# One kernel, all its steps in another order

## The chip, the cores and the metric

The kernel runs on one core of a Trainium2 chip. The metric is the time of one execution in microseconds (us), as the device measures it. Of several executions the median counts.

## What is computed

Three parts follow each other on 8192 tokens of 192 numbers: a local attention over 7 neighbouring tokens, a gated feed-forward layer of width 1536, and a feed-forward layer of width 2048 with a rational activation. Everything is float32 at the outside; the weights arrive as 8-byte numbers.

```python
w = exp(weight_gen - max(weight_gen));  w = w / (sum(w) + 1e-09)      # 8 heads, 7 taps
x1 = sum over k of w[..., k] * x shifted by k                         # 2 x 4096 tokens, 192 wide
x2 = (sigmoid(x1 @ w_gate) * (x1 @ w_val)) @ w_out                    # width 1536
h  = x2 @ w_in                                                        # width 2048
g  = (a0 + a1 h + a2 h^2 + a3 h^3) / (1 + |b0 h| + |b1| h^2 + 1e-06)
out = g @ w_out2
```

## The kernel before

**Tiling.** The tokens are cut into 17 blocks: 15 of 512 tokens and two of 256. A block goes through attention, the first layer (12 units of 128 columns), and the second layer (16 units; the two short blocks take the units in pairs, 6 and 8 of them). Matmuls in the projections run on numbers that are split into a high and a low part, five matmuls for each product of 512 columns.

**Steps and letters.** Each piece of work is a step with a short name. A step does its work on one engine and hands the next step to a waiting list. The lists are first in, first out, so the name says which kind of work comes next, and the list says on which data.

- Weights come in 25 pieces. K loads one with DMAs on SyncE's (SP's) queue; Ka (ScalarE, L183) and Kd (VectorE, L187 to L193) turn the 8-byte words into float32; Kh (ScalarE, L367) and Kl (VectorE, L373) split them; Kc copies the part of the last 64 rows into the tile WT with four DMAs on SP's queue (L217). A projection needs the Kc of its piece.
- X loads a block's inputs on SP's queue; Na, Nb, Nc make the attention weights (Nb is the exponential on ScalarE). Seven steps B (VectorE, L283) make the products of a block, and six steps J or j sum them: **J** lets a transfer add one into the other (a DMA on GpSimd's queue, L430), **j** does it with a VectorE addition (L428). Z (ScalarE) and T1 (TensorE transposes, L459) follow the last of them, then C1 (ScalarE) and L1 (VectorE, L316).
- g and v are the two projections of the first layer into the PSUM banks pg and pv, which exist once each. S (sigmoid, ScalarE) frees pg, M (VectorE, L502) frees pv. G (ScalarE) is the high part of their product; the low part is **L** (a VectorE subtraction, L518) or **l** (ScalarE writes the negative, L515, and a GpSimd DMA adds, L516). O is the projection back. E, E1, E2, C2, L2 turn its sum into the second layer's input; in 14 blocks E2 is again a DMA that adds (L573).
- H is a unit's projection in the second layer (two PSUM banks h). A (three ScalarE instructions), V (L609), W (L614) on VectorE free the bank. **Q** adds two tiles with a GpSimd DMA (L625), **q** with VectorE (L623). R, U (ScalarE), T, Y, D (VectorE, L618), P (TensorE, L673) and F (ScalarE and the output DMA) end the block.

```python
def do_J_j(b, last, x1, to, t, eng):
    ...
    if eng is nc.gpsimd:
        nc.vector.tensor_add(out, out, in_)
    else:
        nc.gpsimd.dma_start(out=out, in_=in_, accum_op=ALU.add)
...
def do_L_l(b, c, g1, gh, eng):
    gl = tl(gp, "gl", [P, T], F32R)
    if eng is nc.gpsimd:
        nc.scalar.activation(gl, g1, AF.Identity, scale=-1.0)
        eng.dma_start(out=gl.bitcast(F32), in_=g1, accum_op=ALU.add)
    else:
        eng.tensor_sub(gl, g1, gh.bitcast(F32))
```

**What sets the order.** One string, ORDER, lists the names of all 3947 steps, and the program issues them in that order. Every engine and every queue works through its own instructions strictly in the order in which they were issued, and waits at one whose data or buffer is not there, whatever stands behind it. The string sets nothing else: buffers rotate as steps ask for them (four r tiles, five v tiles, four q tiles for weights and for the second layer alike).

Of the kernel before, what the change touches and what calls it, by code (L numbers as in the profile page):

```python
# [17 lines left out]
P = 128  # L18
D = 192
# [6 lines left out]
T = P * JB  # L26
# [19 lines left out]
S M K l v E j B g J O E1 M G E2 l G v B S M g C2 l O Kl v Ka S Kd g M Kh v S Kc B Kd K O L2 K g Kd K M Kl G H O G K Ka
L X S v J A g J O G L Z V Ka Ka W l S T1 M C1 G v Ka Kd O L1 Kd M K H H A G g l V v O S Kl Kc A g W H M S B G L g Kd V
v A W V S Q O R L O H U B W Kc B A g M V Q Kd R v H O S M G A Y v W g L G Ka Q U M L T V O S v M H E g W A E1 J v J D
S M Y H V A g Q v G V S W O T B l P E2 R W M H P J G U g L H B A V O A R W v J D Y V P C2 O W S H G l H Kd T M g A G S
P V U W Q g L2 D A H v S G R V L O W O A Na M B Q T V L P H v U Y D J W Y A V P g R S P G M H O A U g v G W S H Nb B L  # L50
P T V W J g D S M A v Nc V H M Z Q L A V W g S Q R v O G P W Y U T1 M X l v T M P C1 L1 O G H l R A D H A P T g V W B
B q S H G V v W A O J V W O Y R M D g G Q H S P v U L B M A g S H A V L v W g Y V T W M G O O D U S P P L R T G J E H
Q L E1 G L Y E2 g R v M H O v S g O A A V W U V S q B M P W D g T G U Y Y C2 J H P S O F A V v L2 H B W A D P P V H Q
G M R g W v L T H B O A G M A P V W R U J D U H S Q V W P L P H T j g l A B A S V W G V v R M Q X Y W P H O H U v D A
g O P R S Y Y T j P G V M L v W g A H M l V W v S G T D U A O Z M V g W v P T1 O G S L T C1 L1 P Q H l H Na R M Y g v
D P G A V U W S A B H O g Q O G D P V M A S G Q W T L B H B P g v V R l U A W V W R J M Y D l H S A V W O v M H Y T g
P G S H A O V A B g S v L W P Q g D U R G M V P W J E E1 Q L F H R v O M H S v T Y A V g W O D U H G S A j B M P U P
E2 L Y B G v Nb O O T L Q A V W P M G V R J P B g C2 L D H A O V G W v S Y W O l H T g P A Q M S H v U g D A S P V W T
V H g W L2 M J H J Y R A U V D v M P G A Q W Nc v S P G H O A T Q Z L M P V V W g v W S T1 P R Y C1 G M D L O L1 O H U
L g G v A X Q B V H L W P B R S Y H g A V M O O U v G A T L V W O H Y S g M R v W S E G g P S U B T D M E1 g L A H q v  # L60
P V G j J A W L O H T D S R E2 B P g Q U O Y G A R V M S v T G W P M L D H V W G L U Y v M O A g P Y H G S L J A v B g
Q M V V F S W W C2 v R O L2 J H A D H B U V P W P A H A M Y Q l V P g W V O P R T S W U H v D B A T J V Y G q G H A W
g M J X P O S T L D P H g V R Z A G W v H Q S M L V O W g U A L V v H P M S D T P R P W G O v U A V Q W T1 Y D G R O
C1 l U L1 T P H A g P B Q V W L B M H H T O S A V g W Y D G O v P B M L A H S R v U A Q O Y M g R S V v G W H J E D Y
P A M l g U V P P W G T S H B V g W E1 Y T Q E2 v Na G l H A V S M g L W R U J O P D G H A D A O V O C2 V W F v W H q
P S g A Y L2 H Q P S M J R V v T W P D A H L O V M U G A L W V v W R M H B Y g T P B J Nb v P S H A g V G D S j M P U
g G W A O v H Q T L S V W A R G B H M v O X Nc L P V U O g P M Q W L H A J G Y R L D v P V S W G A O M T V Q g W v Z
T1 G S Y O D C1 L1 P L l g H B U S M H g A S v A G V T Q g M W Y S R v B H V O D J L R A M P V W g U U W P O T H Y G O
S B A L H D g E G V W Q Y A Q E1 v S P V R H W U g M T P D v M A H R U A J O V L G P W G P Y T V H F O q A W L B P T R
V H v E2 L S A P U D O W M g B H V Y S v A P M g S G V v W H M L g Q J C2 A W v V M G S O g L2 G P H L Q W J v R B Y H  # L70
T O D M S A A G L V V P W O Q B g O P U W T J H D Y v H X R U P Y M A J S v V W A P T H V G D G g Z M Q L W A P V S L
W R v L T1 M Na C1 L1 R B O G P H D U B U Nb A O T O g L T V B J S P Y H v W A G g S Q V O H g Y A M W L S P R V H D v
A O g W D B M Q U E V H R W T v G Y A V J U W P M H Q S P D A H E1 L v g M Y V S v A G R Q V J W L T M B g S G O U P O
v G P Nc W L H A Y g V S L E2 H O A M F g V W G v T L D J M C2 P P S B g H R P D G O W U A V Q H B W T L2 v P L R S G
g A V S U H W g M Y Q A V H O v A R Y W U J P H V W D P T M O v G Q L j A H V G X R U M S D L v Y P A M W P Z g H O L
V v O W A V G W T1 C1 L P S G L1 T Q R P M H O Y g v A G V B H B U J W O Q T H D S M g A V P S g A L L q W v T M S O D
R G P R H O B A g V Y J U P v W P G D P V E W H M L E1 Y l v O G T H S P l A B g V D A M Q W v G S g F V O L H U P W Y
S R g T A H M U V S W v Q D O H g A j B M G v V B W A E2 R C2 S V M Y P J W T H P H B L L2 D O A V W G v L U Q X R g P
O Y G T S A M V H O W v P U A G g L S M H q V G A P j W Q J V g D R W H A Y S v H M V T P A v L P W g H O M Z Na U D V
W Q A O G V P W T S R v T1 L C1 R Y O L M L1 G D P O B H U g H S L G A Y O A B g V W v V H S Q g W P J A M U P T D G H  # L80
V L T R v P W Q A U V R P L H O S Y A M E v W g S D P H Y g V T W M G H P U A V T S W Y Q l A F B v E1 G R H Q U L g M
V W O v O D G E2 M A S V H W v A G O L D g B M L J q S P V Y v B W g T M j O C2 R P U H T O R S A H A B g D J v V V W
G L W G S P U P M L2 H A g J Q Y H A G S R V Q W Y V W v D P H l P B A M O H g j v A R V W T P P M L Q U H S V D v G W
A M T O U Z O g X v S Nb P V Y L W Y G M T1 P D C1 L1 G L O R Nc H g A S Q L V G H T A v U M O L g v S W H O D B T A O
E P M V R Q g W Y V P B v D E1 S J G H g U W A B H A S V R G M V B J W P E2 v P M T J Q L U g S v W H Y L G O C2 B P D
g G H P A M j v V L W L2 S A Y g M H F V T S W Q R D O A V P W v M U T H R A P B V Q W O U H g H G A v L S P L Y O G T
l g A S V Y P W j V g Q R D W U H O P A M G B l V T W H R v U j A D M H P O V S Y v W g H M O P G G D Z v A A V Y V W
W Q P H L R T S O M g A U S v V Q W T1 C1 L O P G M L1 D L H R g H G Y A v S T M V Q U P W O G D L G R P L g H v T A P
O V X W O S A U B E B M Y V L g W S H A V v T g H G Q E1 A S P P W M Q D v V R W B g Y J U H H A J L V Y S A E2 P P G
B O M v W g F V W M H S T v H D O A V M C2 W L L2 G g P S A q J L B D v R P H U G V O M W q G B A g H R U V O P W P A  # L90
T J Y R V H D S G L J v Q P W O H l Y U g T A M Na S v V W G g l A Y V P W S H H R D O T g A L U M Q V R S B v A G P M
J D v W P M V H g A W O Z T O V v W Y G S U T1 P P Nb L C1 Q L1 H M L H R G A g Q l v S O Nc V X W T M G D A O g S v Y
H V G D g O L S W M U B B A V O l E v G g S H M q P v g R J T Y D M R P P U W S G B E1 v H A A V M W Y L V B P W g T O
O S G Q v H M H E2 l U g L G R v A P Y V A W T V O H S P G W D U A M g C2 T V J D W Q F L2 J O H A Y S v R V P L H P W
H A Q U R P B A V W M G g U v H O L V O P D Q S T G B A L W g Y P J M l T S V H W R v A G D V B J P H W U g Q Y A V P
S M H P W A v D H O V A W X J M Q g Y v V W Z T D T1 L O S P M G R B P G P C1 L1 U R H H g T Y U D A O S G L v V W Q M
H A A V g W V v H S P R L B T U L O M W q Y R g B T J O H v Y G A O S L P P V E W A G H E1 D A V M J W g O l q v U S M
# [668 lines left out]
```

## Time and profile before

| what | value |
|---|---|
| median of 3 runs | 1396.8 us (1396.23 to 1398.79) |
| profiled execution, its own time | 1397.84 us |
| its span, first to last instruction | 1396.0 us |
| granted clock of TensorE, mean | 0.989 of full speed |
| instructions | 18221 |

Times below are in us from the span's start. TensorE is PE, its weight load PEld, VectorE DVE, ScalarE ACT, GpSimd POOL. The profile gives for each engine when it worked, how long it idled before an instruction, and what ended the idle time. A matmul of 512 columns overlaps the one before it, so a busy PE is an upper bound of the work it does.

### The profile page before, as it was taken

The numbers are of one execution on the slowest core, as the hardware profiler recorded it, in microseconds if no ns is written. First come the engines' busy times: TensorE is split into PE (matmuls) and PEld (weight loads), VectorE is DVE, ScalarE is ACT, GpSimd is POOL, SyncE is SP. The second block draws the span as 40 slices with busy tenths as digits, with TensorE's granted clock in tenths as the row PEclk, the third lists the DMA queues.
The fourth block names the chain that finished last, engine by engine and source line by source line (L and its number), as shares of the span: only waits on it lengthen the run. The fifth ranks groups of instructions, "written<-read, shape, count | busy, mean of one in ns | idle before, by whom it ended". The sixth has DMA issues, their size and how long they took to land.

```text
span 1396.0 us, 18221 instructions
## 1 busy us (share of the span) xinstructions
PE 1330.1 (95%) x6602; PEld 1150.1 (82%) x6602; DVE 1241.8 (89%) x1654; ACT 1203.7 (86%) x1820; POOL 233.8 (17%) x274
## 2 busy tenths in 40 slices
PE   1788999999999999999999999999999999999987
PEld 0566888888888888878888888888888888899986
DVE  6876998998999898989989999998988999899987
ACT  4665899889889988988989998999898999999985
POOL 1222211112111111111101011110112101211110
PEclk9999999999999999999999999999999999999999
DMA  9998565446535354554626255542555725454452
GB/s 222 236 227 196 100 132 101 84 99 129 111 68 133 72 113 93 106 114 76 142 43 138 48 113 109 94 111 54 101 104 96 146 52 108 83 108 84 95 108 59
DMA packets 59746, 153.82 MB, mean 110 GB/s; under 512 B 7436, under 2 KB 17162, under 8 KB 59656
## 3 DMA queue, kind: packets, MB, share of 16 engines
q0 software_dynamic: 38304, 108.54, 42.7%
q1 hardware_dynamic: 21064, 44.11, 10.4%
q8 instruction: 52, 0.85, 0.3%
q14 instruction: 38, 0.31, 0.1%
q10 hardware_dynamic: 288, 0.00, 0.0%
HBM read 31.51 MB, written 6.29 MB: 27 GB/s over the span
## 4 chain that ended last, share of the span: by engine, by line
PE 49%; DVE 5%; ACT 5%; issue 3%; DMA 2%; POOL 0%; POOLq 0%; ACTq 0%; DVEq 0%
PE acc L673 13%; PE h L295 3%; PE h L296 2%; PE h L297 2%; PE h L298 2%; PE h L299 2%; PE pv L295 2%; PE pg L296 2%; PE pg L295 2%; PE pg L297 2%; PE pg L298 2%; PE pg L299 2%; PE pv L296 2%; PE pv L297 2%; PE acc L533 2%
## 5 line engine op out<-in xcount | busy, mean ns | idle before, releaser
L673 PE MATMUL acc<-wo,v 128*128 128x192 f32 x2048 | 369.8, 327 | 4.1 <-DVE v L618 3.2
L673 PEld LDWEIGHTS acc<-wo,v 128*128 128x128 f32 x2048 | 343.6, 190 | 19.8 <-DVE v L618 4.5
L609 DVE TENSOR_TENSOR v<-v,h 128x512 f32<-128x512 f32 x256 | 174.9, 684 | 82.3 <-ACT r L602 80.8
L600 ACT ACTIVATE v<-h,co 128x512 f32<-128x512 f32 x256 | 176.5, 690 | 44.8 <-PE h L299 40.4
L625 POOL DMA_DIRECT2D q<-r x113 | 104.0, 921 | 604.2 <-ACT r L602 527.1
L614 DVE SCALAR_TENSOR_TENSOR v<-v,co,h 128x512 f32<-128x512 f32 x256 | 189.9, 744 | 3.8
L618 DVE SCALAR_TENSOR_TENSOR v<-v,co,r 128x1024 f32<-128x1024 f32 x128 | 163.3, 1278 | 1.1 <-ACT r L635 1.1
L602 ACT ACTIVATE r<-h 128x512 f32<-128x512 f32 x256 | 155.8, 609 | 2.7 <-DVE q L618 2.4
L601 ACT ACTIVATE q<-h 128x512 f32<-128x512 f32 x256 | 153.4, 599 | 4.7 <-DVE v L618 4.7
L630 ACT ACTIVATE r<-q,co 128x1024 f32<-128x1024 f32 x128 | 147.9, 1156 | 11.1 <-DMA q<-r 8.3
L618 DVE SCALAR_TENSOR_TENSOR v<-q,v 128x1024 f32<-128x1024 f32 x128 | 155.8, 1219 | 0.4
L618 DVE SCALAR_TENSOR_TENSOR q<-q,r 128x1024 f32<-128x1024 f32 x128 | 155.9, 1218 | 0.1
L502 DVE TENSOR_TENSOR sg<-sg,pv 128x512 f32<-128x512 f32 x192 | 130.8, 681 | 26.8 <-PE pv L299 16.4
L490 ACT ACTIVATE sg<-pg 128x512 f32<-128x512 f32 x192 | 116.3, 606 | 38.6 <-PE pg L299 22.1
L635 ACT ACTIVATE r<-r 128x1024 f32<-128x1024 f32 x128 | 136.4, 1068 | 0.9
L508 ACT CAST gh<-sg 128x512 fp32r<-128x512 f32 x192 | 119.4, 626 | 11.1 <-DVE sg L502 9.9
L430 POOL DMA_DIRECT2D x<-pr x78 | 79.2, 1016 | 264.7 <-DVE pr L283 110.3
L295 PE MATMUL h<-X2h,W0h 128*128 128x512 f32 (+1 forms) x272 | 117.0, 430 | 5.7 <-DVE v L614 2.8
L296 PE MATMUL h<-X2l,W0h 128*128 128x512 f32 (+1 forms) x272 | 103.5, 380 | 0.0
L297 PE MATMUL h<-X2h,W0l 128*128 128x512 f32 (+1 forms) x272 | 103.3, 380 | 0.0
L298 PE MATMUL h<-X2h,WT 128*128 128x512 f32 (+1 forms) x272 | 103.2, 379 | 0.0
L299 PE MATMUL h<-X2l,WT 128*128 128x512 f32 (+1 forms) x272 | 102.9, 378 | 0.0
(138 smaller groups left out, 2859.1 us busy)
## 6 DMA issues: line engine op xcount, KB each, us to landing
q<-r POOLq DMA_DIRECT2D x113, 512.0 KB, 4.6
x<-pr POOLq DMA_DIRECT2D x70, 384.0 KB, 5.6
gl<-sg POOLq DMA_DIRECT2D x57, 256.0 KB, 3.8
x<-in_x_dram SPq DMA_DIRECT2D x13, 960.0 KB, 5.5
out_dram<-pr SPq DMA_DIRECT2D x15, 384.0 KB, 3.1
v<-in_moe_w_out_dram SPq DMA_DIRECT2D x14, 384.0 KB, 4.8
r<-r SPq DMA_DIRECT2D x28, 128.0 KB, 2.4
r<-r POOLq DMA_DIRECT2D x14, 256.0 KB, 5.0
```

What stands on the lines that cost most here:

```text
L295: mm(d, W0h[:, w], h[:, 0, :], start=True, stop=False)
L296: mm(d, W0h[:, w], lo[:, 0, :], start=False, stop=False)
L297: mm(d, W0l[:, w], h[:, 0, :], start=False, stop=False)
L298: mm(d, WT[:, w], h[:, 1, :], start=False, stop=False)
L299: mm(d, WT[:, w], lo[:, 1, :], start=False, stop=True)
L600: nc.scalar.activation(v[:, e, :], ph, AF.Identity, scale=reg["a3"], bias=a2)
L601: nc.scalar.activation(q[:, e, :], ph, AF.Square, scale=reg["b1r"])
L602: nc.scalar.activation(a[:, e, :], ph, AF.Abs, scale=reg["b0"])
L609: nc.vector.tensor_mul(v, v, ph)
L614: nc.vector.scalar_tensor_tensor(out=v, in0=v, scalar=a1, in1=ph, op0=ALU.add, op1=ALU.mult)
L618: nc.vector.scalar_tensor_tensor(out=out, in0=in0, scalar=scalar, in1=in1, op0=op0, op1=op1, reverse0=neg)
L673: mm(acc[:, s // 2, (s % 2) * D:(s % 2 + 1) * D], g[:, (e * jb + s) * P:(e * jb + s + 1) * P], wo2[:, c, :], start=(c == 0 and s % 2 == 0) ...
```

## The change

The string ORDER is replaced by another order of the same steps. No function, tile or number elsewhere is touched. The counts of six names change, in pairs: of the block sums 7 go from J to j (82 and 20 before, 75 and 27 now); one low part goes from L to l (135 and 57 before, 134 and 58 now); one sum goes from Q to q (113 and 15 before, 112 and 16 now).

```diff
--- before.py
+++ after.py
@@ -38,75 +38,75 @@
 NB = len(BLOCKS)
 FOLD_PE = (0, NB - 2, NB - 1)
 ORDER = """
-Na Nb Nc K K Na root B B Ka B Ka J K B B B B J j J Kd Kh K J Ka K Kd Kl Ka K Kd Nb Kc Kd Kh Kh j Nc Z Ka X T1 C1 Kh Kd
...
+Na K K Nb Nc root Na B Ka B B B B B Ka K Kd Ka K B K Ka J j K j Kh Kd Kh J Kd Kl Kd Kh Kc Nb Nc Kh J j Kl X Z K T1 Kl
...
 """
```

The order of the instructions that the new string gives shows at three places what moved.

GpSimd's queue at the start of the program, before: four DMAs sum the first block's products (X2l, X2h and pr hold products, x1 the sum), and the low parts gl and the second block's sums follow.

```order
L430 DMA x1_0_138<-X2l_0_140 128x768
L430 DMA X2h_0_145<-X2l_1_156 128x768
L430 DMA X2h_1_158<-pr_1_162 128x768
L430 DMA x1_0_138<-X2h_0_145 128x768
L167 MEMSET x_0_231 128x384
L516 DMA gl_0_341<-sg_0_285 128x512
L430 DMA x1_0_297<-pr_1_318 128x768
L516 DMA gl_1_356<-sg_1_338 128x512
```

The same place now:

```order
L430 DMA x1_0_138<-X2l_0_143 128x768
L430 DMA X2h_1_149<-pr_1_176 128x768
L430 DMA x1_0_138<-X2h_0_145 128x768
L167 MEMSET x_0_231 128x384
L430 DMA x1_0_277<-pr_1_285 128x768
L430 DMA x1_0_277<-pr_0_321 128x768
L516 DMA gl_2_437<-sg_2_395 128x512
```

The sum of products 2 and 3 has left the queue (VectorE does it now), and the first two low parts have left it too.

SP's queue at the pieces of the first layer's last projections, before (v and q tiles are loads of weights, WT the copies of a Kc; WT from r_3_367, r_1_426 and r_3_529 serve units 6 and 7, 8 and 9, 10 and 11):

```order
L225 DMA v_2_429<-in_moe_w_out_dram 128x2x384
L217 DMA WT_81<-r_3_367 64x256 x4
L203 DMA v_3_505<-in_moe2_w_in_dram 128x512
L204 DMA q_3_506<-in_moe2_w_in_dram 64x512
...
L203 DMA v_4_556<-in_moe2_w_in_dram 128x512
L204 DMA q_0_557<-in_moe2_w_in_dram 64x512
...
L217 DMA WT_81<-r_1_426 64x256 x4
L217 DMA WT_81<-r_3_529 64x256 x4
```

The same pieces now (r_3_356, r_1_440 and r_3_514):

```order
L217 DMA WT_81<-r_3_356 64x256 x4
L225 DMA v_2_561<-in_moe_w_out_dram 128x2x384
L217 DMA WT_81<-r_1_440 64x256 x4
L203 DMA v_3_636<-in_moe2_w_in_dram 128x512
L204 DMA q_3_637<-in_moe2_w_in_dram 64x512
...
L217 DMA WT_81<-r_3_514 64x256 x4
L165 DMA x_0_711<-in_x_dram 128x1920
```

The copies for units 8 and 9 stood behind eight loads of the second layer's weights (two pieces of four DMAs) and stand ahead of them now; those for units 10 and 11 stand behind four of them.

VectorE where the second block's attention weights are normalized, before:

```order
L502 TENSOR_TENSOR sg_1_638<-sg_1_638,pv_0_669 128x512
L272 TENSOR_REDUCE red_1_239<-wn_1_238 128x64
L273 TENSOR_SCALAR red_1_239<-red_1_239 128x64
L274 RECIPROCAL red_1_239<-red_1_239 128x64
L275 TENSOR_TENSOR wn_1_238<-wn_1_238,red_1_239 128x448
L502 TENSOR_TENSOR sg_2_706<-sg_2_706,pv_0_710 128x512
```

The same place now:

```order
L502 TENSOR_TENSOR sg_0_608<-sg_0_608,pv_0_610 128x512
L272 TENSOR_REDUCE red_1_239<-wn_1_238 128x64
L273 TENSOR_SCALAR red_1_239<-red_1_239 128x64
L274 RECIPROCAL red_1_239<-red_1_239 128x64
L275 TENSOR_TENSOR wn_1_238<-wn_1_238,red_1_239 128x448
L428 TENSOR_TENSOR x1_0_277<-x1_0_277,pr_0_604 128x768
L502 TENSOR_TENSOR sg_1_632<-sg_1_632,pv_0_662 128x512
```

The second block's last sum is a VectorE addition now, and it stands in front of the step M (L502) that frees the bank pv. It adds to x1, into which a DMA of GpSimd's queue adds just before.

## Rows read from the trace of the kernel before

**Rows 1.** The page, part 1: busy time of each engine, its share, instructions.

```profile
PE 1330.1 (95%) x6602; PEld 1150.1 (82%) x6602; DVE 1241.8 (89%) x1654; ACT 1203.7 (86%) x1820; POOL 233.8 (17%) x274
```

**Rows 2.** Windows: stretch, length, busy time by engine, granted clock, DMA share, GB/s.

```profile
0.00:30.12 30.12, 0.00 (x0) 0.03 (x1) 19.39 (x51) 9.76 (x22) 5.72 (x12) 1.00 0.96 231
30.12:80.00 49.88, 36.75 (x120) 26.88 (x121) 39.35 (x84) 30.18 (x63) 11.55 (x13) 0.88 0.95 223
80.00:140.00 60.00, 55.20 (x227) 43.67 (x227) 44.09 (x83) 37.91 (x72) 13.14 (x15) 0.93 0.88 212
140.00:620.00 480.00, 478.77 (x2313) 411.69 (x2313) 439.01 (x560) 431.45 (x639) 81.91 (x95) 1.00 0.52 104
620.00:640.00 20.00, 17.28 (x81) 14.88 (x80) 16.98 (x23) 15.60 (x22) 2.53 (x3) 0.91 0.47 87
640.00:1300.00 660.00, 658.21 (x3333) 573.62 (x3332) 600.53 (x761) 605.46 (x893) 105.12 (x121) 1.00 0.48 96
1350.00:1396.00 46.00, 35.37 (x208) 32.87 (x208) 35.11 (x39) 26.84 (x39) 3.45 (x4) 0.93 0.34 74
```

**Rows 3.** Timeline of PE: start, length, line, tiles, count, idle before and releaser.

```profile
30.12 1.08 PE L459 MATMUL h<-ident,x 128*128 128x128 f32 x4 [30.12 <-DVE x L428]
...
76.20 0.77 PE L298 MATMUL pg<-X1h,WT 128*128 128x512 f32 x1 [3.77 <-DMA WT<-r]
...
135.07 0.66 PE L459 MATMUL h<-ident,x 128*128 128x128 f32 x4 [2.10 <-DMA x<-pr]
...
627.44 0.63 PE L459 MATMUL h<-ident,pr 128*128 128x128 f32 x4 [2.72 <-DVE v L614]
```

**Rows 4.** Timeline of POOL in the first block: issues of the summing DMAs.

```profile
13.39 0.86 POOL L430 DMA_DIRECT2D X2h<-X2l  x1 [0.72 <-DVE X2l L283]
...
22.43 0.86 POOL L430 DMA_DIRECT2D x<-X2h  x1 [4.72 <-DMA X2h<-X2l]
```

**Rows 5.** Timeline of DVE in the first block, and the low part for units 8 and 9.

```profile
13.86 1.82 DVE L283 TENSOR_TENSOR pr<-x,wn 128x768 f32<-128x768 f32 x2
15.60 0.95 DVE L428 TENSOR_TENSOR X2h<-X2h,pr 128x768 f32<-128x768 f32 x1
16.47 0.42 DVE L187 TENSOR_SCALAR r<-r 128x256 uint32<-128x256 uint32 x2
...
17.88 0.35 DVE L187 TENSOR_SCALAR r<-r 128x384 uint32<-128x384 uint32 x1
...
23.36 0.41 DVE L193 SCALAR_TENSOR_TENSOR r<-q,r 128x256 uint32<-128x256 uint32 x1
29.02 0.96 DVE L428 TENSOR_TENSOR x<-x,X2h 128x768 f32<-128x768 f32 x1 [5.24 <-DMA x<-X2h]
29.89 0.38 DVE L272 TENSOR_REDUCE red<-wn 128x32 f32<-128x224 f32 x1
...
31.22 0.35 DVE L187 TENSOR_SCALAR r<-r 128x384 uint32<-128x384 uint32 x1
...
63.50 0.42 DVE L373 TENSOR_TENSOR r<-r 128x256 f32<-128x256 f32 x1
```

**Rows 6.** Waits over the whole span: who waited for whom, total, times, longest.

```profile
PE pg L298 <- DMA WT<-r: 8.7, 4, 3.8
```

**Rows 7.** Timeline of SP's queue before the copies for units 8 to 11.

```profile
59.20 1.67 SPq L203 DMA_DIRECT2D v<-in_moe_w_in_dram  x1
...
68.22 7.44 SPq L217 DMA_DIRECT2D WT<-r  x8
```

**Rows 8.** The copies into WT (L217), issue to landing: shortest, median, longest.

```profile
DMA to landing us min/median/max: 1.8/4.1/7.8
```

**Rows 9.** DMA issues by line: count, size of one, median time to landing.

```profile
x<-pr POOLq DMA_DIRECT2D x70, 384.0 KB, 5.6
gl<-sg POOLq DMA_DIRECT2D x57, 256.0 KB, 3.8
```

**Rows 10.** Groups of instructions by line: busy, mean ns of one, idle before and releaser.

```profile
L428 DVE TENSOR_TENSOR x<-x,pr 128x768 f32<-128x768 f32 (+1 forms) x18 | 15.5, 863 | 2.9 <-DMA x<-pr 2.9
```

More of the change, by code (lines that the diff above doesn't have):

```diff
@@ L46 @@
[L46 to L95, printed above, removed]
@@ new lines @@
+Ka Kd Ka C1 L1 Kd B g B Kc v S g Kh Na Kh M K Nb Kl B G Ka Kl v S K Kc L O Kd Kl Ka g K M J G Kh v B Kc Kd S Ka M Kh g
+L S v K Kd G g J O l Ka S M Kl Kl g Kd v J G Kh M Kl l O Ka Kh v K G S Kd l Kc Ka g O M Kl B v S g Kh J Kd O K G M Kh
+S Ka B G v Kc Kl g L O Kl M B L S v g Kd M Nc J j S G K l Kc O g S v M G g Ka v Z S Kd T1 O X M K L C1 L1 G v G O Kh L
+l M g G v S B g O Ka l B Kh j M Kl S Kl G K v B g M O B S g L v S Kd M J Kc Ka Kd O G Kh g G K S L l v O K E M E1 G B
+g v S E2 O g C2 j Ka M v L L2 J B M Kl Kh H G S K l Ka Ka O g G J Kd l K S K v B Kc O M Kd K g S v O Kl Ka M A g V v
@@ new lines @@
+Ka j Z G O S W T1 C1 Kd g G Ka K M L Kc v L1 H S A L H O Kd M A V g S W O G Kd V H G Kh W A v g L X L H Q M S G Kd v g
+A O S V R M V v W B H g Kl U G O M A Q B v W L V O H R U W Y Kc H M Q S v L g O A G S T D M v G E V L G l g M A E1 O W
+v J Y H L V S g P M P G B L v Q Na Ka W R S H T O A E2 g U B M A v D O P V G T Y V C2 J W S M O g D H Q R Kd P U W l T
+J R S v Y A H A U V W B g P K G Q O Ka G J D H P M G S V A v W B g V L H Y J M O L S R W g P A S T P V D H Q v U g Kd
+G P W B l J H l L2 A M v O A V W T P H M S Y Nb D G V W A Z V O v R P L G P W Q T1 C1 O M Nc X G O L1 R U H g K L L S
@@ new lines @@
+Ka B v T H Y M g v A V G U S W A B O O T M E g S V v Q D Y H M g v A W G Q P S g Kd R E1 U G J E2 B L D V H P L A W T
+M R O S P H V P J L v W g Y A F O V G S W M U H A g G H L D Y A S v T Q V V P P W H R W Q D B B U H A M j J A g R P V
+C2 v L S O W V H G U M T W l Y L2 v A D O V g G M W O H B P B S H A V Q g P W A H S R U g A G J T V L Y v O W H M V W
+Q v l R D H P q T M J Y U R A O P V G S X W v D P A M H A V L g v O Z W G V W T T1 Q P S Y U P C1 G O D R L1 B H g M H
+B S L T v L g M Y A U S V W O A v g J G G H Q S P Y g M l D V A B q R R P U V W v P M W T H U O A J H B l O J Y v V A
@@ new lines @@
+A G g S R U V T Y W D H v M E2 A Y Q l V T g H P A W v C2 J V R L2 W O M O G H P D v U L G A V M B S P j H P A g Y S Q
+B W O v R V H L W T U Y Q P O M H G A g V W v A O V W S M H v T D P R j g M Q j G A Z P U v G V R W T1 D L P C1 L O L1
+T S H A H g A V U L P W V Y H X Q W S O g M P A H B S G V D O v R A B W g G Y H Q l U P M V T W v J A D R G P L M B H
+v S A V O Y g W V O M U T S L H E g G A J Q v P Q P B E1 S W L H Na T D J V W R U G L Y F A O g O H M V P T A W V D v
+P M R G S Y W L U B G H O v g O E2 T Q M A C2 S H P v B Nb V A Y P M g W R V D L2 H U v A P J W S H L P V g Y W A D H
@@ new lines @@
+M Q B G S A v V G g L J T R W O Q O G X V P M S v W H P L l D Nc A j Z g G V S H O A U M V v W W Y Q g R M P G T L U
+T1 v P D C1 R O L1 H H S A A O g L Q S B G V W U M H P V v A T l Q g P W Y S H T M B G L V W g D B Y R D U v H M A A P
+O G O O J v R Y V S W E V J P G H g W M T H v L U A E1 L A B P Q S D O M V G W V g G v P W Q S M H L Y g E2 R O T F J
+R S P v l M B U g G H P B A J v S T V A V O W D W C2 L G g Y M l S H O A H Q L2 U V O D W g P A H V v B Q G W P Y S T
+R M P H U D g A R V v T O l W U G Y A H S P M v P V A W j X V G D W O M H g j Na A G H L Z L V S W Q P v P M A Q V W O
@@ new lines @@
+L g v T1 R Y G R U C1 S O T D L1 O U Y H L M H P A g A S v Y V W O B H P G T P g Nb D M V B W P H Q A R V v B S W j L
+A M J V G H T g Q A W S O B U v E V M g Q S E1 P T G L G D v Y H R g O U W D L P P J M Nc A R L H v S V O W M g A F H
+G V v S T g Y W O U H A S G M L v g V q O P E2 A B B V C2 Y M l S g R G J D P T l W S v P H U W A M Q B H Y J g G V D
+P W S A O V L2 P v l H T W R j D G O U M H L v Z A P A V Q R W Y T H U g M P S A v V W D T O H P X V A G W H V g M Q A
+q V v S W R W P T1 L O C1 Y O G M U G L1 H D P B g v B L P R l S G H T U O Y M A A J V g W G H L l v S A T B q B O V M
@@ new lines @@
+L M H S A T V A O g j v Q G W F H j P M U O V G D L2 S T v B P W A g M V G R Q L S H W Y l A U v H J P V O A W g Na V
+M T S W L Q P D H g R v O G H B A P B R J O M v L O U P Y V S J W Y H M G l g D P G A V T U W X Q A V W D l H S v T G
+Nb A P Z H O A Y Q V W M V g v R W T1 C1 P L P S Nc G U L1 M H H D g A B V v A O W Q S H V O g T M W G P v A Y L B Q S
+B V R R U W M H g O J P v L J G R D T H Y A O V P S W A P U B l D G l V M B g H P S v g j W H G T E Y D U A P V S A g
+M W E1 T v O S H V F g O G M W Y L A q v G O S M H v P g L R Q G D J P V A E2 U W V M R W U H T S v H Y g B D M A Q V
@@ new lines @@
+P W C2 A J O Q V L S l H B W R O v T J P H L2 U Y M G A G R g V W D P L T v S Y A P M H V U O W A l D g G P H V q S l
+A W P v H T V g A S V O X P W M G v W Z R q T1 C1 P Y M U L1 O D l G R l B H g P T S U A Y D Q V H A W O g G v O H S V
+P W L M T A g H v S V Y g W B R A M G U D H O V Q R B P v J A U L W P H P Y A S M G Q T V J P O l v W V H E W G D g H
+Y T E1 A O M S g V F Q W Na B E2 A L v G O M H S R B A V L v G O V M U W R g q O H J W S Y P v g T L U T G M D Y Nb S
+B H P A G O D g S V C2 v P P L M A D G W l v V g P M R H W O L2 U L Y S T A V J W H A v V B g W D j S Q P R g G H H U
@@ new lines @@
+S W H B Q M P g V U W Y A L P H B v O D S T R O U G V W Q B H M P Y v L A g Y P V W M A R D v T S E U V g W S H Y J G
+H A g M v L V A S E1 q T O R E2 V P G W j g P O G l H U l M B D W Q F G L A v H M Y P v S g V J W M C2 O A H Q D P T
+L2 S V B R B W G g A O H U v G P O l A V R W Y D T P H U S V W T A Q H D V P A O Y J P R W M V g H U W B S A j T G Q Y
+H X v P M L V g v W A O V P H S J R D A G M L W Z v D M g V U P v W T L Q T1 P R O C1 L1 G B S H P B A j B V W J l H g
+B Y A H V P S W O M U G g H O v A Q D V T Q L Y G O S W D R A U g V M J H Y v l B R W A M B S J P G U H v l P G q V A
@@ new lines @@
+g W S T O H M J T g E P v P D Y E1 V A V S W H R U G A L M v B W j Q D O g R V M v Z W E2 T1 F U C1 L T S L1 Y P H P H
+A G Y V W Q g C2 D A S H V A T W P V W R P H H D L2 O A P P Q A U M V L W V H W R T H g G A v Y V U D W A Q R V L P S
+W H P Q H g T A Y A P V M W S U V P D R O H A O W Y U T Q D V H W Y A V Q P P v G H G L W T R O l U M D A H V T A V O
+P W G R E P W H U Q L Y H E1 A V P W A R g V E2 D P C2 W U S L2 v Q H F H Y g T A P A T V M Q P W S V H R W D Y A H D
+A U Q R v V P G M P V W W U T v l H Y T H g O A V M A R V W Y W P S P H H U D D P A Q v A V T P W R G V Y H W A P D U
@@ L110 @@
+V Q H M A R W Q P T V H A U W O H P Y G V D l P W A T V H Y P R Q l O U W A H D P V G Y l O W A R V T U W H O H D O A
+P A T Q E V V W R E1 E2 W C2 L2 P H U Y F T H Q D A V P A V R P W U H W H Y A P Y P V Q W A V Q D W R T H A H A V U D
+P V P W W H Q R A Y T V D H A W U V P Q T Y P R F U P P T Y D P W P R D U T Y P P D P P F
 """
```

33 lines of the change are left out of this document (15 added, 18 removed).

## The prediction

> **What bounds the kernel now.** The page's first part comes first: PE is busy in 1330.1 of 1396 us, DVE in 89%, ACT in 86% [rows 1]. An order can therefore give back at most what PE loses, and the windows say where that is [rows 2]. PE does nothing until 30.12. From 30 to 80 us it idles 49.88 − 36.75 = 13.1 us, and the granted clock of 0.88 costs (1 − 0.88) × 49.88 = 6.0 us more. From 80 to 140 us the two losses are 4.8 and 4.2. Then 480 us follow with 1.2 us of idle time, a dent at 620 to 640 us (2.7 idle, 1.8 by the clock), 660 us with 1.8, and an end from 1350 us with 10.6 idle. So 99.7% of the long middle is already full, and what an order can win lies in the first 140 us, in the dent and in the end. The granted clock is a mean of two levels, 2.4 and 1.2 GHz; it is below 1.00 only in the stretches where PE also idles, and I read it as following the idle time.
>
> The same view shows what is full early on: DMA engines are 0.95 busy from 30 to 80 us and 0.88 from 80 to 140 (223 and 212 GB/s), about 0.5 afterwards. DVE has room there: 49.88 − 39.35 + 60 − 44.09 = 26.4 us idle [rows 2].
>
> Next I read PE's timeline and the list of waits for the releasers [rows 3, 6]. The first transposes wait for VectorE's last sum of block 1. Four times, 8.7 us in all, a projection waits for the copies into WT, the longest 3.77 us at 76.20 for unit 8. The third block's transposes wait 2.10 us for a summing transfer at 135.07, and the dent is a wait of 2.72 us before transposes, too.
>
> **First block: −2.7 us.** Before, the sums of products 2 and 3 were a transfer, issued at 13.39; POOL then stood 4.72 us waiting for it, issued the last sum at 22.43 [rows 4], and DVE could add at 29.02, after 5.24 us of idleness [rows 5]. PE started 1.1 us behind that. Now DVE adds 2 and 3 itself. DVE's products end at 13.86 + 0.87 = 14.73, if the two of 1.82 us follow the same stream. The new list has one pack of a weight piece among them (16.47 to 17.88, so 1.41 us), one product more, and two additions of 0.87: 14.73 + 1.41 + 0.87 + 1.74 = 18.75. POOL issues the first of its two last transfers about then and the second some 0.9 us later, at 19.7, which is 2.7 us before 22.43. The landing takes as long as it did, 29.02 − 22.43 = 6.6 us, so 26.3. DVE meanwhile has the other packs (17.88 to 23.77, 5.9 us) and the normalization of the weights (29.89 to 31.22, 1.33 us) to do: 18.75 + 5.9 + 1.33 = 26.0. They just fit. If they overrun, the gain sinks to half, −1.4; if POOL is quicker, −3.0.
>
> **Waits of PE from 30 to 140 us: −11 us.** The loss there is 13.1 + 6.0 + 4.8 + 4.2 = 28.1 us, the ceiling of this term; its other end is nothing. Three parts:
>
> The copies for unit 8. Their source was ready at 63.50 + 0.42 = 63.9 [rows 5], yet SP issued them only at 68.22, since eight loads of the second layer's weights, from 59.20 on, stood ahead in its queue [rows 7]. In the new order they stand ahead of those loads. The 4.3 us exceed the wait of 3.77, so I take all of it: −3.8.
>
> The other three waits (8.7 − 3.8 = 4.9 us) and the one of 2.10 before the third transposes are landings while the DMA engines are full. A copy of WT lands in 1.8 us at best, 4.1 in the median, 7.8 at worst [rows 8]. The change lightens this stretch. Up to the third block's transposes the old order has 15 J and 17 l, the new one 11 and 9. At 384 and 256 KB [rows 9] that is 5.8 + 4.4 = 10.1 MB before and 4.2 + 2.3 = 6.5 MB now; a difference of 3.6 MB is 16 us of all DMA engines at 223 GB/s [rows 2]. Weight pieces called for by then go from 24 to 22. I take half of those waits, 0.5 × (4.9 + 2.1) = −3.5.
>
> Less idle time leaves the clock up more often: I take 4 of its 10.2 us, the share of the named waits (7.3 of 17.9 us of idleness): −4. Together −11.3.
>
> VectorE pays for the lighter transfers: four j at 863 ns [rows 10], and six or so more low parts, each on 512 columns and so below the price of that addition of 768: at most 10 × 0.863 = 8.6 us, against 26.4 idle. I cost it at nothing; without the cover it would be those 8.6 us.
>
> **The dent at 627 us: −2 us.** These transposes read what a block's last sum has filled [rows 3]; the row names a W (L614) as the last thing that ended on DVE ahead of them. In the order of before, the last summing transfer of the tightest block has a single group of PE's work between itself and the transposes; now at least five stand between in every block. Of 2.7 + 1.8 = 4.5 us I take not quite half, bounds 0 and −4.5.
>
> **The rest of the engines.** DVE gains seven j (7 × 0.863 = 6.0 us) and one q, and loses one L, which about cancel; it idles 1396 − 1241.8 = 154 us [rows 1]. ACT loses ten table loads by the new list (154 to 144) and idles 192 us. Neither sets the end, hence nothing. The end itself has the same steps behind the last second-layer input in both orders, so its 10.6 idle us stay: 0.
>
> **Allowance: +3 us.** 3947 steps move, and the waits of PE in the old order sum to 1.2 and 1.8 us in the two long stretches [rows 2]. A new order can hardly undercut that, and may add as much again.
>
> Sum: −2.7 − 11.3 − 2 + 3 = −13.0. Against the profiled execution's 1397.84 that gives 1384.8; the median of the runs is 1.04 lower, hence 1384.
>
> **Rivals.** What a measurement tells from no change here is 0.2%, 2.8 us.
>
> *A, the sum above*: 1375 to 1390. At 1390 the clock (4) and the dent (2) give nothing. At 1375 the other half of the named waits goes as well (3.5), the dent wholly (2.5), and the allowance isn't needed (3).
>
> *B, the transfers of GpSimd's queue never held the copies.* Then only the first block and the copies for unit 8 win, −2.7 and −3.8, and the allowance takes a part: −3 to −8, about 1391. For it speaks that the DMA engines stay full with loads anyway: SP has as much to load as buffers come free. Against it, that the copies' landings spread from 1.8 to 7.8 us [rows 8], more than fourfold, in a stretch at 0.95 busy. Here the Trainium skill has a rule, in "DMA: Bandwidth & Descriptors", section "Queues, rings and completion order": each DMA engine goes round the queue rows that have work, one packet at a time. By it, another queue can at most halve the share of SP's queue, and a copy mostly waits behind loads of its own queue; the sum by that rule alone would be B's, about 1391. The trace's factor of 4 is more than a halving, so loads ahead in the same queue must have part in it, but it doesn't say how much is the other queue's.
>
> *C, what the start wins is lost again* in the middle by waits elsewhere: within ±2.8 us of 1396.8. The middle is full, and a gain at the start can only be kept if later transfers are as early as the steps are. For it speaks that each of the 14 blocks can bring one dent like the one of 627 us (4.5 us): two or three of them eat the gain.
>
> *D, slower: VectorE's additions wait for transfers.* A j that adds to a tile into which a transfer has just been added waits for that landing, 5.6 us in the median [rows 9], at the head of DVE's in-order queue. Behind it stand M, V and W, which free pv and the two banks h, so PE stops within a unit. In the list above the second block's last sum is just that, directly in front of an M. Before, 18 such additions waited 2.9 us together [rows 10], since they stood far enough behind the transfer. There are seven more j: if all found it in flight, 7 × 5.6 = 39 us. It decides as soon as more than 13 / 5.6, that is two to three full landings, are not covered. I put it at 1400 to 1408. Against it: 2.9 us over 18 additions is 0.16 us for one, so nearly all of them found their data there, and a landing of 5.6 us is short beside the tens of us that a block takes.
>
> **How the numbers follow.** A 0.48, B 0.22, C 0.12, D 0.18. A and B are faster by more than 2.8 us: 0.70; C the same: 0.12; D slower: 0.18. The likeliest is A, 1384. The range of 8 in 10 takes in A and B, C's part up to 1399 and a tail below: its ends are A's 1375 and C's 1399. D lies above it and is left out.
>
> **What would show it.** The first transposes at about 27.4 instead of 30.12. PE's waits for WT below 4 us in all, none near 3.8 at unit 8. The third transposes ten us or so before 135.07, nearer 124, and a granted clock above 0.93 in most of 30 to 140 us. In the middle no wait before transposes (L459) of over 1 us. The forecast is wrong if DVE's waits at L428 for summing transfers grow from 2.9 to more than ten us, if the waits for WT stay near 8.7 us (B), or if PE's idle time from 140 to 1300 us grows by more than 5 us (C).

## The result, and the profile of the changed kernel

The changed kernel takes 1367.15 us (median of 4 runs, 1365.17 to 1367.64); before, the median of 4 runs beside them is 1396.71. The ratio is 0.9783, with a 95% interval of 0.9766 to 0.9800: 30 us faster, more than twice the 13 that were forecast, and below the range given (1375 to 1399). The profiled execution has a span of 1365.9 us.

First the page's first part and the windows, as in [rows 1] and [rows 2]; the last window is again the last 46 us of the span.

```profile
PE 1313.3 (96%) x6602; PEld 1144.3 (84%) x6602; DVE 1246.6 (91%) x1661; ACT 1193.4 (87%) x1811; POOL 226.9 (17%) x267
```

```profile
30.12:80.00 49.88, 40.94 (x162) 30.77 (x163) 45.73 (x93) 30.17 (x60) 7.76 (x9) 1.00 0.95 233
80.00:140.00 60.00, 60.00 (x262) 49.38 (x262) 54.65 (x96) 45.06 (x86) 8.86 (x10) 0.97 0.65 151
140.00:620.00 480.00, 476.22 (x2314) 411.08 (x2313) 438.35 (x559) 435.39 (x641) 83.35 (x96) 1.00 0.54 108
...
640.00:1300.00 660.00, 659.25 (x3395) 581.00 (x3394) 609.79 (x767) 604.59 (x903) 109.05 (x126) 1.00 0.48 96
1320.00:1365.90 45.90, 35.22 (x218) 33.57 (x218) 35.76 (x41) 26.70 (x40) 3.52 (x5) 0.96 0.35 75
```

PE idles 8.9 us from 30 to 80 us (13.1 before) and not at all from 80 to 140 (4.8); the granted clock is 1.00 and 0.97 there, 0.88 and 0.93 before. From 640 to 1300 us it does 3395 matmuls, where it did 3333, with the same busy time.

The timeline of PE, its first transposes and all its waits for transfers over 1 us; the list of waits over the span; the copies into WT:

```profile
27.99 1.09 PE L459 MATMUL h<-ident,x 128*128 128x128 f32 x4 [27.99 <-DVE x L428]
...
55.38 0.50 PE L534 MATMUL acc<-gl,O0h 128*128 128x512 f32 x1 [1.20 <-DMA gl<-sg]
...
79.67 0.65 PE L534 MATMUL acc<-gl,O0h 128*128 128x512 f32 x1 [3.21 <-DMA gl<-sg]
```

```profile
PE acc L534 <- DMA gl<-sg: 4.8, 4, 3.2
...
PE pv L295 <- DVE sg L502: 3.1, 4, 1.1
```

```profile
DMA to landing us min/median/max: 1.9/3.7/7.7
```

The four waits for WT, 8.7 us in [rows 6], are gone, and so is the one before the third transposes in [rows 3]. What PE still waits for is another transfer, that of a low part (L516) in front of the matmul that reads it (L534). The copies themselves land hardly sooner: 1.8, 4.1 and 7.8 us in [rows 8].

Since a busy PE hides short waits, I also measured its lateness: at a matmul, the time since the span's start, less what all matmuls ahead of it would take at the usual (median) spacing that the trace shows for their kind (227 ns for 512 columns, 120 for 256, 162 for L673, 109 for a transpose; 1294 us for all 6602). The same amount of work stands in one row whatever the order:

```
us of work done      before   after   lateness won in this stretch
0 (first matmul)       30.1    28.0    2.1
100                    64.8    45.1   17.6
500                    69.9    49.7    0.5
560                    74.9    53.1    1.6
1260                   84.3    57.3    5.2
end of the span       101.8    71.6    3.2
```

So 20 of the 30 us come from the first 100 us of work (165 us of time before, 145 now), and 10 from behind it, where the prediction had a loss of 1 in sum (+3 and −2).

### The profile page after: what moved, and what is told of

Its sections match the earlier page's. It is cut to its first block, busy times and chain, and to the rows that moved or that the text cites. A ratio compares the mean times of both kernels' runs of the same rounds, so it can differ in the third digit from the quotient of the medians.

```text
span 1365.9 us, 18184 instructions
## 1 busy us (share of the span) xinstructions
PE 1313.3 (96%) x6602; PEld 1144.3 (84%) x6602; DVE 1246.6 (91%) x1661; ACT 1193.4 (87%) x1811; POOL 226.9 (17%) x267
## 5 line engine op out<-in xcount | busy, mean ns | idle before, releaser
L673 PE MATMUL acc<-wo,v 128*128 128x192 f32 x2048 | 369.1, 327 | 4.0 <-DVE v L618 2.1
L673 PEld LDWEIGHTS acc<-wo,v 128*128 128x128 f32 x2048 | 342.9, 190 | 18.8 <-DVE v L618 2.6
L625 POOL DMA_DIRECT2D q<-r x112 | 104.7, 935 | 550.9 <-ACT r L602 472.8
L502 DVE TENSOR_TENSOR sg<-sg,pv 128x512 f32<-128x512 f32 x192 | 130.6, 680 | 19.8 <-PE pv L299 16.7
L516 POOL DMA_DIRECT2D gl<-sg x58 | 50.9, 877 | 322.3 <-ACT gl L515 244.1
L430 POOL DMA_DIRECT2D x<-pr x72 | 71.7, 995 | 186.7 <-DVE pr L283 77.6
L298 PE MATMUL h<-X2h,WT 128*128 128x512 f32 (+1 forms) x272 | 102.7, 377 | 0.0
```

The source lines that it names most:

```text
L502: nc.vector.tensor_mul(g1, g1, pv)
L673: mm(acc[:, s // 2, (s % 2) * D:(s % 2 + 1) * D], g[:, (e * jb + s) * P:(e * jb + s + 1) * P], wo2[:, c, :], start=(c == 0 and s % 2 == 0) ...
```

## The experiments

All kernels are permutations of the same steps, or the same order with other choices of engine, unless said. "The start" is what stands up to the third block's transposes; 14 choices differ there (4 J became j, 9 l became L, one L became l). Each time stands beside runs of the kernel before on the same chip (medians of 1395.3 to 1396.5); 1.000 is no change. Differences from the changed kernel are taken from the medians; by the ratios they come out up to 3 us otherwise.

**The start alone.** The new order's first 806 steps, then the others as before stood.

```diff
-(first 806 steps of before)
+(first 806 steps of the new order)
 (all other steps, in the order of before)
```

> The first 806 steps in the new order (to just behind the fifth block's transposes, some 210 us), the other 3141 in the order of before. The traces put 19 of the 30 us before 140 us: first matmul 2.1 earlier, and 17 less lost by TensorE from 30 to 140 us. If that is how it is, 1377 us, with the dent near 620 us and the end of before still there. If the later gain is also a consequence of the start (transfers that come earlier all along), about 1368.

Measured 1382.3 us, 0.9903 (0.9886 to 0.9919), 13 us faster than before and slower than either expectation. The lateness at 100 is 47.6, so 17 of the start's 20 us are there; behind it, up to 1260, this kernel loses 23 us where before loses 19, the stall before the ninth block's transposes included. So the later gain isn't a consequence of the start: it belongs to the rest of the string.

**The choices alone, the places alone.** Two kernels: the order of before with the 14 choices of the start, and the new order with the choices of before in the start.

```diff
 (order of before)            (new order)
-J l  (4 J, 9 l, one L)      -j L
+j L                         +J l
```

> The order of before; only the 14 engine choices up to the third block's transposes are those of the new order (4 J become j, 9 l become L, one L becomes l). The prediction's theory (software transfers hold the copies into WT): 8 to 12 us faster, TensorE's waits for WT well under 8.7 us. The rival (SP's own queue holds them): only the first block's 2 us, waits for WT as before, near 1394; the additions may also wait for transfers there and cost a few us.

> The new order with the 14 engine choices of before up to the third block's transposes, so that its software transfers are as many as before there. The prediction's theory: half or more of the early gain goes, 1376 to 1380, with waits for WT again. The rival: the first block's 2 us and little more, 1369 to 1371.

Measured 1398.0 (1.0016, 1.0005 to 1.0028) and 1394.0 (0.9993, 0.9984 to 1.0003): neither is worth anything without the other. The second is even 6 us later than before at 100 us of work (71.0 for 64.8), and the rest of its string wins that back. PE's waits for transfers, in the first and in the second:

```profile
PE pg L298 <- DMA WT<-r: 6.6, 4, 3.4
...
PE acc L534 <- DMA gl<-sg: 4.8, 2, 4.1
...
PE h L459 <- DMA x<-pr: 0.8, 1, 0.8
```

```profile
PE acc L534 <- DMA gl<-sg: 15.9, 7, 7.0
...
PE h L459 <- DMA x<-pr: 6.5, 2, 3.6
```

With the new choices in the old places the copies hold PE nearly as before, as the rival expected, and one VectorE addition waits 9.0 us for a sum, which may be why the time lies above the rival's 1394. With the old choices in the new places no copy holds PE, though as many transfers of GpSimd's queue run; but it waits 15.9 us for low parts and 6.5 for block sums. The prediction's theory expected waits for WT to come back here, and they didn't; both of this run's times missed. PE is also up to 15 us later here than in the changed kernel (60.2 for 44.9 at 50 us of work), which gives the copies time, so this run alone doesn't clear the transfers; the next ones do more.

**Low parts or sums.** The new order with the choices of the start undone by kind: the 10 low parts, or the 4 sums.

```diff
 (new order)                  (new order)
-L  (9 of the first 20)      -j  (4 of the first 18)
+l  (and one L for an l)     +J
```

> The new order with the 10 low parts up to the third block's transposes made as before (nine of them by a transfer again, one by VectorE); the four sums stay with VectorE. If it is TensorE's second-layer groups (O) that must not wait for a transfer, nearly all of what the 14 choices are worth in this order goes here: 1385 to 1392, waits for gl as in the run with all 14 (15.9 us). If it is the load on the DMA engines, the bytes count: 9 x 256 KB of 3.9 MB, so some 60% of it.

> The new order with the four block sums up to the third block's transposes made by transfers as before; the low parts stay as in the new order. By TensorE's dependence: the first block (1.3 us) and the waits before the second and third blocks' transposes (6.5 us in the run with all 14) come back, with the clock 1375 to 1378. By the load on the DMA engines: 40% of the 27 us, about 1378, with waits for gl too.

Measured 1381.2 (0.9903, 0.9887 to 0.9920) and 1374.8 (0.9847, 0.9830 to 0.9863), 14 and 8 us over the changed kernel. Of transfers, PE waits for gl alone in the first and mostly for a sum in the second:

```profile
PE acc L534 <- DMA gl<-sg: 17.9, 7, 6.8
```

```profile
PE h L459 <- DMA x<-pr: 5.5, 1, 5.5
...
PE acc L534 <- DMA gl<-sg: 1.5, 2, 1.1
```

The times alone don't decide: 14 us is less than PE's dependence was expected to cost and near the 60% of the load, and 8 us fits either. What speaks for the dependence is what PE waits for. No copy holds it in either run, in the second not even up to 80 us, where PE is about 2 us later than in the changed kernel.

**The load put back.** Behind each of the 13 steps that became VectorE work, GpSimd's queue also issues a transfer of that size that nobody waits for (ZJ and ZL). It copies from DRAM to DRAM and adds nothing, so it stands for the bytes of the old transfers, not for their kind.

```diff
+    def extra(cols):
+        nc.gpsimd.dma_start(out=spare[u, :, 0:cols], in_=...)
-... j ... L ...
+... j ZJ ... L ZL ...
```

> The new order; behind each of the 13 steps of the start that became VectorE work (4 sums, 9 low parts) GpSimd's queue also issues a transfer of the same size that nothing waits for (input to a spare array in DRAM, 3.9 MB in all). If the lighter load on the DMA engines is what the start gains from (the prediction's reason), the waits come back: 1375 to 1385. If it is that TensorE no longer waits for those transfers: within 3 us of the changed kernel's 1367.

Measured 1365.1, 0.9769 (0.9748 to 0.9789): as fast as the changed kernel. The windows from 30 to 140 us, the landing of the copies, and PE's wait for them (the lines' numbers are one higher here):

```profile
30.12:80.00 49.88, 42.32 (x166) 30.48 (x164) 46.91 (x95) 30.82 (x61) 11.23 (x15) 1.00 0.96 249
80.00:140.00 60.00, 58.33 (x249) 47.98 (x250) 52.55 (x93) 42.21 (x81) 11.53 (x15) 0.94 0.78 196
```

```profile
DMA to landing us min/median/max: 1.8/4.8/10.2
```

```profile
PE pg L299 <- DMA WT<-r: 1.1, 2, 0.6
```

The load is really there (249 and 196 GB/s for 233 and 151), and the copies do land later, 4.8 us in the median for 3.7. But PE feels 1.1 us of it. Its lateness at 100 is 48.2, 3 us more than the changed kernel's; those 3 us are regained later by the absence of another wait (below). So the load of bytes has at most 3 of the 20 us. The margin is thin, though: in the changed kernel the copies that the gate projections of units 2, 4, 6, 8 and 10 read land only 0.8 to 2.9 us ahead of the matmul (L298) that reads them.

**Loads and copies moved alone.** K and Kc where the other order has them, counted in groups of PE's work: in the order of before, and the other way round in the new order.

```diff
 (order of before)               (new order)
-K, Kc as before                -K, Kc as in the new order
+K, Kc as in the new order      +K, Kc as before
```

> The order of before, with its engine choices; only the weight loads (K) and the copies (Kc) stand where the new order has them, counted in TensorE's groups of work, as far as buffers and data allow. The rival: the waits for WT go (8.7 us) and with them part of the 10 us that the clock costs, so 10 to 14 us faster, about 1385. The prediction's theory: the copies for unit 8 only, 4 to 5 us, about 1392.

> The new order, in which the weight loads (K) and copies (Kc) stand where the order of before has them, counted in TensorE's groups of work (a few Ka, Kd and others come with them where buffers need it). If the places on SP's queue are a part of the gain that the engine choices can't bring: waits for WT come back, 5 to 9 us and some clock, 1374 to 1380. If with few software transfers the copies land in time anyway: 1367 to 1370.

Measured 1414.3 (1.0128, 1.0110 to 1.0147) and 1387.4 (0.9939, 0.9918 to 0.9960). No expectation held either time. In the first, the waits for WT fall as the rival said, and others come:

```profile
PE acc L534 <- DMA gl<-sg: 5.6, 3, 3.9
...
PE h L459 <- DMA x<-pr: 4.7, 2, 2.9
...
PE pg L298 <- DMA WT<-r: 3.0, 2, 2.3
```

Its lateness at 60 is 59.0 against 60.3 before: 5.7 us of waits for copies removed, 1.3 won. The loss comes after 140 us: a Ka (L183) waits 9.3 us on ScalarE for the load right ahead of it, which now comes later, and PE waits 8.1 us for ScalarE's S. The second kernel is 7 us later than the changed one at 100 and another 11 at 150; the waits for WT are only 3.0 of it. Some Kd and Ka of the last pieces had to come along there, and from 100 to 200 us ScalarE's A waits four times, 7.5 us in all, for the last VectorE instruction (L193) of such a Kd. So neither run prices SP's queue by itself.

**The first block's sum.** The new order with one J back, that of products 2 and 3.

```diff
-... K Ka J j K j Kh ...
+... K Ka J J K j Kh ...
```

> The new order; only the sum of the first block's products 2 and 3 is a transfer again. The first block's term by itself: first matmul at about 30 instead of 28.0, 2 us slower than the changed kernel, 1369. If what comes behind waits for transfers anyway: 1367.

Measured 1366.5, 0.9781 (0.9760 to 0.9803): no difference. The first matmul moves to 29.4, and the lateness stays 2.8 us above the changed kernel's up to 500 us of work. At 560 it is 52.6 for 53.1. The changed kernel has a wait of 1.81 us there, at 599 us, that this run and the run with the extra load don't have. It starts on ScalarE, where an R waits for a sum that was issued at 579.63, right after SP's load of a block's inputs:

```profile
579.26 0.33 SPq L165 DMA_DIRECT2D x<-in_x_dram  x1
...
579.63 0.86 POOL L625 DMA_DIRECT2D q<-r  x1 [5.94 <-DVE pr L283]
...
588.37 1.15 ACT L630 ACTIVATE r<-q,co 128x1024 f32<-128x1024 f32 x1 [4.08 <-DMA q<-r]
```

That transfer took 8.7 us, where 4.6 is the median of its kind. In the run with one J back and in the one with the extra load, the sum goes 1.6 us ahead of that load (580.45 and 582.02, 580.97 and 582.56) and lands in 5.2 us. The run with one J back also shows the slow rival's mechanism once: VectorE waits at the head of its queue for a sum's landing, the M behind it is late, and PE waits for the bank.

```profile
77.05 0.96 DVE L428 TENSOR_TENSOR x<-x,pr 128x768 f32<-128x768 f32 x1 [3.58 <-DMA x<-pr]
```

```profile
78.66 0.79 PE L295 MATMUL pv<-X1h,W0h 128*128 128x512 f32 x1 [3.12 <-DVE sg L502]
```

**Where the choices' gain went in the old order.** 11 of the 14 choices; the last sum and two low parts just ahead of the third transposes stay as before.

```diff
 (order of before)
-J l  (3 J, 8 l)
+j L
```

> The order of before with 11 of the 14 choices: the last sum and two low parts just ahead of the third block's transposes stay as before. The run with all 14 was 8.6 us ahead of before until that place and lost it there. If that loss is of these three choices, this is 1386 to 1388. If it is of later transposes in general, 1393 to 1396.

Measured 1393.0, 0.9976 (0.9966 to 0.9987). It is 6.8 us ahead of before at 500 us of work (the lateness is 63.1 for 69.9), of which the ninth block's transposes take back 2.3:

```profile
617.73 0.63 PE L459 MATMUL h<-ident,x 128*128 128x128 f32 x4 [0.47 <-DMA x<-pr]
...
621.97 1.08 PE L459 MATMUL h<-ident,pr 128*128 128x128 f32 x4 [3.61 <-DVE v L614]
```

So the three choices do cost most of what the run with all 14 lost there (the lateness at 100 is 58.0, and 63.5 with all 14), but the stall near 620 us takes part of it back.

**The clock.** In the order of before, PE repeats the first matmul of three groups, about as long as it then waits for the copies; every repeat is overwritten.

```diff
+            for _ in range({2: 6, 4: 12, 8: 16}.get(unit, 0) if b == 0 and o == 0 else 0):
+                mm(d, W0h[:, w], h[:, 0, :], start=True, stop=True)
             mm(d, W0h[:, w], h[:, 0, :], start=True, stop=False)
```

> The order of before; ahead of the first block's units 2, 4 and 8 TensorE repeats the first matmul of the group 6, 12 and 16 times (1.4, 2.7 and 3.6 us at full speed; each repeat is overwritten by the real one), about what it then waits for the copies. If the clock falls because of the idle time and its 7 us there are lost time: 4 to 7 us faster. If the transfers set the pace and what the clock costs is waited away at the next landing: within 2 us of before, or slower by what a repeat overruns.

Measured 1399.5, 1.0021 (1.0007 to 1.0034). The clock from 30 to 80 us rises from 0.88 to 0.93:

```profile
30.12:80.00 49.88, 43.07 (x156) 32.29 (x155) 38.83 (x82) 29.34 (x63) 11.31 (x13) 0.93 0.94 226
```

The second, third and fourth block's transposes come 1.6, 2.0 and 1.7 us sooner than before, 0.5 us of which the first matmul brings. So of the (0.93 − 0.88) × 49.88 = 2.5 us of clock some 1.2 arrive, and the next transfers are waited for all the longer (4.78 us before the third transposes, 2.10 before). By the last block's transposes it is 1.9 us behind, which I didn't follow further; the run speaks for transfers that set the pace there, but doesn't settle what the clock costs.

**Choices and places behind the start.** 107 choices differ there. The new order with those of before, the order of before with the new ones, and the new order with the end (from step 3554 on) of before.

```diff
 (new order)             (order of before)      (new order to step 3554)
-choices of new         -choices of before     -(end of new)
+choices of before      +choices of new        +(end of before)
```

> The new order; behind the third block's transposes the engine choices are those of before (107 of them differ: 16 J were j, 30 L were l and so on, nearly as many each way). The traces put some 10 us of the gain behind 140 us. If the choices make it, that goes: 1375 to 1380. If the places of the steps make it, within 2 us of the changed kernel's 1367; choices that were fitted to other places can also cost more than 10.

> The order of before with the new order's engine choices behind the third block's transposes. If the choices alone bring the later gain: 1386. If they need the new places: 1396 or slower.

> The new order up to step 3554 (behind the last block's transposes, some 1215 us), then the order of before. The traces put 3 us of the gain behind that place (a wait of 2.25 us for a copy on ScalarE, and the clock, are gone). If so: 3 us slower than the changed kernel, 1370. If the end only lies otherwise: 1367.

Measured 1419.6 (1.0166, 1.0147 to 1.0185), 1471.1 (1.0535, 1.0517 to 1.0553) and 1372.0 (0.9821, 0.9803 to 0.9839). Mixing costs 52 us over the changed kernel and 75 over the one before, though nearly as many choices go each way; no expectation held that much, beyond the word that choices fitted to other places can cost more than 10. In the first of them PE waits for low parts, and ScalarE for sums and low parts:

```profile
ACT r L630 <- DMA q<-r: 27.1, 11, 4.9
...
ACT sg L490 <- DMA gl<-sg: 22.7, 9, 5.8
...
PE acc L534 <- DMA gl<-sg: 17.8, 9, 3.7
...
DVE x L428 <- DMA x<-pr: 4.7, 2, 4.3
```

The new end gives 4.8 us by the medians, 2.5 by lateness behind 1260.

**Two more low parts on VectorE.** The new order; the third and eighth low parts of the program, for which PE still waits, become L.

```diff
-... G g J O l Ka S ...
+... G g J O L Ka S ...
-... S G K l Kc O g ...
+... S G K L Kc O g ...
```

> The new order, in which two more low parts (the third and the eighth of the program) are subtractions on VectorE. TensorE waits 1.20 and 3.21 us for their transfers in the changed kernel, and the clock halves for 3.4 us behind the second. If what it waits for is the transfer and VectorE has room: 4 to 6 us faster than the changed kernel, 1361 to 1363. If the next late transfer takes the place: within 2 us of 1367.

Measured 1358.6 us (1357.5 to 1359.8), 0.9733 (0.9716 to 0.9749): 8.5 us faster than the changed kernel by the medians (7 by the ratios), more than expected, and the fastest of all. No PE wait for a transfer is left from 30 to 140 us, and the clock is full:

```profile
30.12:80.00 49.88, 44.48 (x177) 33.26 (x178) 49.31 (x99) 32.41 (x65) 6.89 (x8) 1.00 0.90 224
80.00:140.00 60.00, 60.00 (x271) 49.77 (x270) 56.37 (x98) 46.36 (x84) 8.63 (x10) 1.00 0.69 159
```

The lateness at 100 is 40.1 for 45.1, which is the 4 to 6 us expected; 3.3 us more are the wait at 599, which is absent here too (the sum goes 1.6 us ahead of the load here as well).

## Why the prediction was right or wrong

**First block.** Right in mechanism, and in size: the first transposes came at 27.99 for 30.12, 2.1 us where 2.7 were forecast. Undoing that one addition moves the first matmul by 1.4 us (29.39) and leaves the kernel 2.8 us later up to 500 us of work, but gives no measurable time in the end, since the wait at 599 us is absent in that run. So no run shows what the term is worth in the whole.

**Waits from 30 to 140 us.** This step failed, in its reason and its size. Its reason was that 3.6 MB fewer bytes let the copies land sooner. They land nearly as before (median 3.7 us for 4.1); putting 3.9 MB back changed no time and cost PE about 3 us on the way; and with as many transfers as before, no copy held PE in the new places, though it came later there. What happened has two parts. The copies stopped holding PE because of where the steps stand, for all four and not just the one that the prediction named; which of the steps' places does it, the runs don't separate. And low parts and sums that stand close ahead of their use are no longer transfers. That can be counted in the two orders: of the first 18 low parts, the old order has 16 by transfer, with 5.4 groups of PE's work (steps of PE, mostly of five matmuls) on average between the step and the O that reads it. The new one has nine by transfer with 5.2 groups, and nine on VectorE with 2.2. With the old choices in the new places, eight of the 18 and the twentieth are transfers with 3 groups or fewer, and all seven waits of that run, 15.9 us, are at these. A transfer of that kind lands in 3.8 us in the median [rows 9], and a group of five matmuls takes 1.1 us. The distance isn't all: the longest wait that is left in the changed kernel, 3.21 us, is at the eighth low part, which has 6 groups. Its transfer was issued at 71.09, among SP's load of a block's inputs (67.31) and eight loads of weights (67.69 to 73.88), and landed in 8.5 us.

Rival B was nearly right about the transfers of GpSimd's queue, and wrong about the sum, since it saw nothing else that could win. The Trainium skill's rule behind it ("DMA: Bandwidth & Descriptors", section "Queues, rings and completion order": the engines go round the queue rows packet by packet) agrees with the run in which 3.9 MB on the other queue made the copies 1.1 us slower in the median, 4.8 us for 3.7, which is less than the halving that the prediction worked out from it; the slowest copy took 10.2 us for 7.7.

The size: the term took half of the waits that it didn't explain and 4 of the 10.2 us of clock. All four waits went, and the clock gave back 10.2 − 1.8 = 8.4 us (0.03 × 60 = 1.8 is left). The 17.6 us won up to 100 us of work stand for the 11.3 forecast, and the third block's transposes started at 117.61, not near 124. The range's lower end, 1375, held neither the rest of the clock nor any gain in the middle and at the end.

**VectorE's share at no cost.** Right: its idle time from 30 to 140 us shrank from 26.4 to 9.5 us, and it didn't hold PE there longer than 1.1 us at a time, 3.8 us in all from 30 us on (4.9 before).

**The dent, the allowance and the end.** Forecast −2, +3 and 0; measured −1.6, −5.2 (with −0.5 earlier) and −3.2. The dent of before is gone, and another of 1.8 us stands near it, behind a sum that was issued right after SP's load of a block's inputs and landed late. The allowance was wrong in sign. I read 99.7% busy as "nothing to gain", but busy time holds waits that are shorter than a matmul's own record: 660 us with the same busy time hold 62 matmuls more, if not of quite the same mix. By the runs with mixed choices, places and choices must fit there as well; which of the many short waits made the 5 us I didn't separate. The end was put at nothing because the same steps stand there; they stand in another order, and with the end of before put back 2.5 of the 3.2 us are lost again.

**The slow rival** didn't happen in the changed kernel: VectorE's additions wait 0.6 us for transfers in all. Its mechanism showed elsewhere: such additions wait 3.6 us in the run with one J back, 9.0 with the choices alone, 5.3 with the old low parts and 4.7 in the first run with mixed choices.

## What to carry to other kernels

Where work can go to an engine or to a transfer, the choice and the place are one decision: count how much work stands between the step and its reader, and give the short distances to the engine. Then look at what else is being loaded when a transfer is issued, since that can make a long distance too short. Undoing or taking over half of such a change tells little about the whole; here 14 choices alone were worth nothing, and the new order without them nothing, while in the new order they are worth 27 us. When an engine is 99% busy, compare how much work it has done by a certain time, not how long it was busy.

## What the runs showed of the hardware beyond that

The 3.9 MB that were added to a stretch with DMA engines 0.95 busy cost PE some 3 us there and left the kernel's time as it was: they moved 249 GB/s instead of 233, at 0.96.

A single large load beside a summing transfer costs it more. Behind 140 us of the changed kernel, the five sums of the second layer (L625, 512 KB) that were issued within 1 us of SP's load of a block's inputs (L165, 960 KB) landed in 8.0 to 10.2 us. The 94 sums with no such load issued from 7 us ahead of them to 6 us behind landed in 4.6 us in the median and 7.4 at most. One of the five is enough to stop PE for 1.8 us at 599; in the three runs where that sum went 1.6 us ahead of the load, it landed in 5.2 us and the wait was absent. No run moved such a load by itself, so this is read from the traces and not tested.
